# A third PSUM bank pair for the first six score steps, the result added in place, and a remade instruction order

## The chip, the cores and the metric

The kernel runs on one core of a Trainium2 chip. The metric is the time of one execution in microseconds (us), measured on the device. A run also reports the mean clock that TensorE was granted, and a profile shows one execution in detail. Runs marked slow (more than 1.5% above the fastest of their kernel) are left out of every comparison and are named where they occur.

TensorE is called PE below, its weight loads PEld, VectorE DVE, ScalarE ACT, GpSimd POOL, and SyncE SP.

## The reference

Attention in which a query sees only keys of its own hash bucket, followed by a layer norm and a two-layer MLP with a residual:

```python
q_bits = einsum('bhsd,dk->bhsk', q, proj) > 0        # 6 hash bits; the same for k
mask   = bucket(q)[..., None] == bucket(k)[..., None, :]
scores = where(mask, q @ k.T / sqrt(D), -1e9)        # B 4, H 8, S 768, D 64
attn   = softmax(scores)                             # + 1e-9 in the denominator
x      = (attn @ v).transpose(0, 2, 1, 3).reshape(B, S, 512)
xn     = (x - mean) / sqrt(var + 1e-6) * g_ln
out    = x + relu(xn @ w_ch1) @ w_ch2                # 512 -> 2048 -> 512
```

## The kernel before

The program is a list of words. Each is `name.engine.arguments`, and the kernel issues them in exactly that order; each engine takes its own words in order and waits, by semaphores, for data and for free buffers.

```python
for word in ORDER.split():
    name, eng, *args = word.split(".")
    OPS[name](ENGINES[eng], *map(int, args))
```

The attention is cut into 72 steps `s` = 0 to 71: 12 blocks `u` of 256 query rows, two groups of four heads, and three parts of the keys. A step is a score step S (24 matmuls), two exponentials E, and a value step A (16 matmuls). Three steps fill one accumulator, which DVE then normalises into `x` (words `na`, `nb`, `nc`). Two accumulators make a block, whose layer norm (`ce`), transposes (`ft`, `fc`), first MLP layer (F, eight pairs of columns), ReLU (R) and second layer (D, quarters of the hidden size) follow.

```python
def sc(s, h):                       # scores of one half (two heads): two banks
    return ps(f"sc{s}{h}", [P, 2, 512], ("scA", "scB")[h])
def S_(eng, s, h):                  # h = 2: all four heads, both bank pairs
    ...
                    nc.tensor.matmul(sc(s, i // 2)[:, i % 2, ...], lh, rh, ...)
def E_(eng, s, h):
    nc.scalar.activation(E(s)[:, heads(h)], sc(s, h), AF.Exp, scale=EXP_SCALE, bias=bias_sb)
def A_(eng, s, h):
    ...
    acc = ps(f"acc{u}{g}", [P, 2, 512], "acc")
    ...
def warm(eng):                      # 46 matmuls on ones, for the clock
    wp = ps("warm", [P, 2, 512], "acc")
    ...
def pf(eng):                        # the projection, spread over a weight tile
    for i in range(4):
        nc.vector.tensor_copy(pfull[32 * i : 32 * i + 32, :, 32 * i : 32 * i + NB], prj)
def lw1(eng, n):                    # one of eight weight loads (four of each layer)
    nc.gpsimd.dma_start(out=w1_sb[:, :, 512 * n : 512 * n + 512], in_=w1ap[:, :, 512 * n : 512 * n + 512])
```

The kernel's PSUM tiles take eight banks: the pairs `scA`, `scB` and `acc`, and one bank each for `f1` and `f2` (hashes and MLP). A hash group is `tn` (DVE transposes), `ha` (four fp32 matmuls) and `bi` (DVE makes the bits). The list begins:

```
mem.v warm.t lp.a lx.s.0.1.1.3 pmem.p p32.p tn.v.0.1.2 pf.v ha.t.0.1.2 ca.p.0.1.2 lx.s.0.0.0.1 tn.v.0.0.0 ha.t.0.0.0
on.p.1 ca.a.0.0.0 lx.s.0.1.0.1 tn.v.0.1.0 ca.a.0.1.0 lv.s.1.0.0 bi.v.0.1.2 ha.t.0.1.0 bi.v.0.0.0 S.t.2.1 E.a.2.1
S.t.2.0 E.a.2.0 ... S.t.0.1 S.t.0.0 ... S.t.1.1 E.a.1.1 S.t.1.0 ...
```

The softmax here doesn't subtract the row's maximum and nothing guards it: scores larger than these inputs give would overflow.

Of the kernel before, what the change touches and what calls it, by code (L numbers as in the profile page):

```python
# [17 lines left out]
mem.v warm.t lp.a lx.s.0.1.1.3 pmem.p p32.p tn.v.0.1.2 pf.v ha.t.0.1.2 ca.p.0.1.2 lx.s.0.0.0.1 tn.v.0.0.0 ha.t.0.0.0  # L18
on.p.1 ca.a.0.0.0 lx.s.0.1.0.1 tn.v.0.1.0 ca.a.0.1.0 lv.s.1.0.0 bi.v.0.1.2 ha.t.0.1.0 bi.v.0.0.0 S.t.2.1 E.a.2.1
S.t.2.0 E.a.2.0 lx.s.1.0.0.1 tn.v.0.1.1 ca.p.0.1.1 ha.t.0.1.1 tn.v.1.0.0 ca.v.1.0.0 bi.v.0.1.0 S.t.0.1 S.t.0.0  # L20
E.a.0.1 E.a.0.0 ha.t.1.0.0 bi.v.0.1.1 S.t.1.1 E.a.1.1 S.t.1.0 E.a.1.0 lv.s.0.0.4 cv.p.0.0.2 sa.p.0.0.2 sa.p.0.0.1
cv.p.0.0.0 lx.s.1.1.0.3 tn.v.1.1.0 tn.v.1.1.1 ha.t.1.1.0 tn.v.1.1.2 ca.a.1.1.2 sa.p.0.0.0 bi.v.1.0.0 lv.s.1.0.3
bi.v.1.1.0 LX.s.1.0.0 tu.v.1.0.0.3 lg.s on.p.0 A.t.2.1 A.t.0.1 A.t.0.0 ca.p.1.1.0 S.t.3.2 E.a.3.1 E.a.3.0
tu.v.1.0.0.1 ha.t.1.1.1 bi.v.1.1.1 tu.v.1.0.0.2 CA.a.1.0.0.1 ha.t.1.1.2 bi.v.1.1.2 A.t.2.0 ca.p.1.1.1 S.t.4.2
E.a.4.0 lx.s.0.0.1.3 tn.v.0.0.1 sb.p.0.0 su.p.0.0 sp.t.0.0 sc.v.0.0 lw2.p.3 A.t.1.1 tn.v.0.0.2 ha.t.0.0.1 bi.v.0.0.1
lw1.p.3 ca.p.0.0.1 A.t.1.0 na.v.0.0 nb.v.0.0 nc.v.0.0 E.a.4.1 S.t.6.2 E.a.6.0 ha.t.0.0.2 bi.v.0.0.2 lv.s.0.4.4
cv.p.0.4.0 cv.p.0.4.2 A.t.4.2 A.t.3.2 sa.p.0.4.0 sa.p.0.4.2 sa.p.0.4.1 sb.p.0.4 su.p.0.4 lw1.p.0 E.a.6.1 S.t.5.2
E.a.5.0 lx.s.1.0.1.3 tn.v.1.0.1 ca.p.1.0.1 tn.v.1.0.2 ha.t.1.0.1 bi.v.1.0.1 LX.s.1.0.1 tu.v.1.0.1.3 tu.v.1.0.1.1
tu.v.1.0.1.2 LX.s.1.1.0 ha.t.1.0.2 LX.s.2.0.1 bi.v.1.0.2 sp.t.0.4 sc.v.0.4 E.a.5.1 S.t.7.2 E.a.7.1 E.a.7.0 A.t.5.2
na.v.0.1 S.t.8.2 E.a.8.1 E.a.8.0 nb.v.0.1 A.t.7.2 nc.v.0.1 ce.v.0.0 ft.t.0.0 A.t.6.2 ce.v.0.1 ft.t.0.1 fc.a.0.1  # L30
S.t.9.2 E.a.9.1 E.a.9.0 tu.v.1.0.1.0 LX.s.1.1.1 fc.v.0.0 F.t.0.1 F.t.0.6 R.a.0.1 R.v.0.6 A.t.8.2 S.t.10.2 E.a.10.1
E.a.10.0 lw1.p.1 F.t.0.3 F.t.0.2 R.a.0.2 na.v.1.0 nb.v.1.0 A.t.9.2 nc.v.1.0 CA.p.1.0.1.1 lw2.p.0 ca.v.0.0.2 S.t.11.2
E.a.11.0 E.a.11.1 tu.v.1.0.0.0 hm.t.1.0 bt.v.1.0 mo.s.1.0.2.0 mo.s.1.0.3.0 mo.s.1.0.2.1 mo.s.1.0.0.0 A.t.10.2
lv.s.1.0.1 R.v.0.3 ca.v.1.0.2 CA.a.1.0.1.0 tu.v.1.1.0.1 mo.s.1.0.2.2 S.t.13.2 E.a.13.1 E.a.13.0 A.t.11.2 na.v.1.1
nb.v.1.1 nc.v.1.1 ce.v.1.0 fl.s.1.0 lw1.p.2 F.t.0.5 R.v.0.5 F.t.0.4 R.a.0.4 S.t.14.2 E.a.14.0 E.a.14.1 lw2.p.1
F.t.0.0 R.a.0.0 lw2.p.2 A.t.13.2 ce.v.1.1 fl.s.1.1 F.t.0.7 R.v.0.7 mo.s.1.0.1.3 mo.s.1.0.1.0 lv.s.1.4.0 mo.s.1.0.3.3
lv.s.1.0.2 sa.p.1.0.1 sa.p.1.0.2 cv.p.1.0.2 CA.a.1.0.0.0 tu.v.1.1.1.0 tu.v.1.1.1.3 tu.v.1.1.1.2 mo.s.1.0.0.3 rs.p.1
S.t.12.2 E.a.12.1 E.a.12.0 D.t.0.0.0 D.t.0.0.1 D.t.0.0.2 rs.p.0 tu.v.1.1.0.3 F.t.1.2 R.v.1.2 S.t.16.2 E.a.16.1
lv.s.1.4.3 mo.s.1.0.2.3 mo.s.1.0.0.2 mo.s.1.0.0.1 F.t.1.1 R.a.1.1 lv.s.1.4.1 mo.s.1.0.3.2 tu.v.1.1.0.0 mo.s.1.0.1.1
A.t.12.2 E.a.16.0 mo.s.1.0.1.2 mo.s.1.0.3.1 A.t.14.2 tu.v.1.1.0.2 CA.a.1.1.0.1 tu.v.1.1.1.1 hm.t.1.1 bt.v.1.1  # L40
mo.s.1.1.0.3 mo.s.1.1.3.1 mo.s.1.1.0.0 mo.s.1.1.1.2 mo.s.1.1.1.1 mo.s.1.1.0.2 mo.s.1.1.2.2 S.t.15.2 E.a.15.0
E.a.15.1 F.t.1.0 R.v.1.0 D.t.0.0.3 F.t.1.7 R.a.1.7 S.t.17.2 E.a.17.0 E.a.17.1 CA.p.1.1.1.1 F.t.1.5 lv.s.1.4.2
LX.s.2.0.0 na.v.2.0 nb.v.2.0 A.t.16.2 nc.v.2.0 A.t.15.2 Z.v.0.0 mo.s.1.1.3.3 mo.s.1.1.1.3 R.v.1.5 F.t.1.3 R.a.1.3
A.t.17.2 na.v.2.1 nb.v.2.1 nc.v.2.1 ce.v.2.1 fl.s.2.1 ce.v.2.0 fl.s.2.0 mo.s.1.1.0.1 S.t.18.2 E.a.18.0 E.a.18.1
mo.s.1.1.1.0 mo.s.1.1.2.0 F.t.1.4 R.a.1.4 D.t.0.1.0 D.t.0.1.1 D.t.0.1.2 D.t.0.1.3 S.t.19.2 E.a.19.0 mo.s.1.1.2.3
mo.s.1.1.2.1 F.t.1.6 R.a.1.6 Z.v.0.1 D.t.1.0.0 D.t.1.0.1 E.a.19.1 mo.s.1.1.3.0 F.t.2.3 R.a.2.3 cv.p.1.4.2 S.t.20.2
E.a.20.0 CA.v.1.1.0.0 tu.v.2.0.1.1 tu.v.2.0.1.2 tu.v.2.0.1.0 tu.v.2.0.1.3 CA.a.2.0.1.1 cv.p.1.0.0 A.t.19.2 E.a.20.1
mo.s.1.1.3.2 F.t.2.2 R.v.2.2 D.t.1.0.2 D.t.1.0.3 O.s.0.1 O.s.0.2 CA.p.1.1.1.0 tu.v.2.0.0.0 tu.v.2.0.0.1 sa.p.1.0.0
sb.p.1.0 lv.s.2.0.2 su.p.1.0 sa.p.1.4.1 sp.t.1.0 sc.a.1.0 LX.s.2.1.1 on.p.2 cv.p.1.4.0 rs.p.2 S.t.23.2 E.a.23.1
E.a.23.0 F.t.2.4 R.v.2.4 lv.s.2.0.0 A.t.18.2 A.t.20.2 na.v.3.0 lv.s.2.0.1 F.t.2.5 R.a.2.5 O.s.0.0 S.t.21.2 E.a.21.0  # L50
E.a.21.1 lv.s.2.0.3 Z.v.1.0 D.t.1.1.0 nb.v.3.0 nc.v.3.0 F.t.2.1 A.t.23.2 R.v.2.1 S.t.22.2 E.a.22.0 E.a.22.1
sa.p.1.4.2 sa.p.1.4.0 sb.p.1.4 su.p.1.4 sp.t.1.4 sc.v.1.4 lv.s.2.4.0 lv.s.2.4.1 A.t.21.2 D.t.1.1.1 tu.v.2.0.0.3
LX.s.2.1.0 F.t.2.0 R.v.2.0 S.t.24.2 E.a.24.1 CA.v.2.0.0.0 E.a.24.0 A.t.22.2 na.v.3.1 cv.p.2.0.0 LX.s.3.0.0
tu.v.2.0.0.2 LX.s.3.0.1 lv.s.2.4.3 lv.s.2.4.2 F.t.2.6 R.v.2.6 D.t.1.1.2 S.t.28.2 E.a.28.0 E.a.28.1 cv.p.2.0.2
CA.v.2.0.0.1 F.t.2.7 R.a.2.7 D.t.1.1.3 nb.v.3.1 nc.v.3.1 ce.v.3.1 A.t.24.2 fl.s.3.1 S.t.25.2 E.a.25.1 E.a.25.0
ce.v.3.0 fl.s.3.0 cv.p.2.4.0 Z.v.1.1 O.s.1.0 O.s.1.3 O.s.1.1 O.s.1.2 hm.t.2.0 tu.v.2.1.0.1 bt.v.2.0 mo.s.2.0.2.3
mo.s.2.0.2.1 mo.s.2.0.0.1 mo.s.2.0.1.1 tu.v.2.1.0.2 tu.v.2.1.0.0 CA.a.2.1.0.0 mo.s.2.0.1.2 mo.s.2.0.0.2 mo.s.2.0.2.2
D.t.2.0.0 D.t.2.0.1 mo.s.2.0.3.2 mo.s.2.0.0.0 mo.s.2.0.3.3 S.t.26.2 E.a.26.1 E.a.26.0 O.s.0.3 mo.s.2.0.1.3 D.t.2.0.2
D.t.2.0.3 Z.v.2.0 sa.p.2.0.1 F.t.3.2 R.a.3.2 A.t.25.2 CA.a.2.0.1.0 tu.v.2.1.1.0 tu.v.2.1.1.1 S.t.29.2 E.a.29.1
E.a.29.0 cv.p.2.4.2 A.t.26.2 F.t.3.5 R.a.3.5 tab.a na.v.4.0 nb.v.4.0 nc.v.4.0 tu.v.2.1.1.3 D.t.2.1.0 D.t.2.1.1  # L60
S.t.27.2 E.a.27.1 E.a.27.0 F.t.3.0 R.v.3.0 mo.s.2.0.3.0 tu.v.2.1.0.3 CA.a.2.1.0.1 LX.s.3.1.1 D.t.2.1.2 A.t.29.2
F.t.3.3 R.a.3.3 S.t.31.2 E.a.31.0 sa.p.2.0.0 sa.p.2.0.2 lv.s.3.0.0 lv.s.3.0.1 D.t.2.1.3 Z.v.2.1 lv.s.3.0.2 F.t.3.1
R.v.3.1 mo.s.2.0.2.0 A.t.28.2 A.t.27.2 na.v.4.1 nb.v.4.1 nc.v.4.1 ce.v.4.0 E.a.31.1 S.t.30.2 E.a.30.1 E.a.30.0
ce.v.4.1 rs.p.4 fl.s.4.1 F.t.3.7 R.a.3.7 D.t.3.0.0 D.t.3.0.1 rs.p.3 S.t.32.2 E.a.32.0 E.a.32.1 O.s.2.2 F.t.3.6
R.v.3.6 A.t.30.2 A.t.31.2 fl.s.4.0 mo.s.2.0.0.3 F.t.3.4 S.t.34.2 mo.s.2.0.3.1 mo.s.2.0.1.0 tu.v.2.1.1.2 CA.p.2.1.1.1
R.v.3.4 hm.t.2.1 bt.v.2.1 mo.s.2.1.0.1 mo.s.2.1.1.3 mo.s.2.1.2.3 mo.s.2.1.3.3 mo.s.2.1.1.1 tu.v.3.0.0.3 mo.s.2.1.2.2
tu.v.3.0.0.1 E.a.34.0 D.t.3.0.2 F.t.4.5 R.v.4.5 E.a.34.1 A.t.32.2 O.s.2.0 S.t.33.2 E.a.33.0 E.a.33.1 F.t.4.7 R.v.4.7
D.t.3.0.3 Z.v.3.0 F.t.4.1 R.a.4.1 S.t.35.2 E.a.35.0 E.a.35.1 mo.s.2.1.3.2 O.s.2.1 na.v.5.0 nb.v.5.0 nc.v.5.0
D.t.3.1.0 D.t.3.1.1 tu.v.3.0.0.0 mo.s.2.1.1.0 lv.s.3.0.3 F.t.4.3 R.a.4.3 mo.s.2.1.0.0 CA.v.3.0.0.0 A.t.35.2
mo.s.2.1.0.2 S.t.36.2 E.a.36.1 E.a.36.0 tu.v.3.0.0.2 CA.a.3.0.0.1 F.t.4.4 R.v.4.4 mo.s.2.1.0.3 mo.s.2.1.3.1  # L70
mo.s.2.1.1.2 mo.s.2.1.2.0 A.t.34.2 A.t.33.2 mo.s.2.1.3.0 mo.s.2.1.2.1 F.t.4.2 R.a.4.2 S.t.37.2 E.a.37.0 D.t.3.1.2
D.t.3.1.3 F.t.4.0 E.a.37.1 S.t.38.2 E.a.38.0 E.a.38.1 na.v.5.1 nb.v.5.1 A.t.37.2 on.p.3 nc.v.5.1 ce.v.5.0 fl.s.5.0
ce.v.5.1 rs.p.5 fl.s.5.1 A.t.36.2 Z.v.3.1 O.s.3.0 O.s.3.1 O.s.3.3 O.s.3.2 LX.s.3.1.0 R.v.4.0 F.t.4.6 R.v.4.6
D.t.4.0.0 CA.p.2.1.1.0 tu.v.3.0.1.3 S.t.39.2 E.a.39.1 tu.v.3.0.1.0 tu.v.3.0.1.1 CA.p.3.0.1.0 F.t.5.0 R.v.5.0
D.t.4.0.1 D.t.4.0.2 D.t.4.0.3 Z.v.4.0 E.a.39.0 S.t.40.2 E.a.40.0 E.a.40.1 F.t.5.4 R.v.5.4 D.t.4.1.0 A.t.38.2
sb.p.2.0 su.p.2.0 sp.t.2.0 sc.a.2.0 sa.p.2.4.0 sa.p.2.4.1 sa.p.2.4.2 lv.s.3.4.2 na.v.6.0 nb.v.6.0 nc.v.6.0 S.t.41.2
E.a.41.1 F.t.5.6 R.a.5.6 sb.p.2.4 su.p.2.4 D.t.4.1.1 D.t.4.1.2 lv.s.3.4.3 F.t.5.5 R.v.5.5 E.a.41.0 A.t.41.2 S.t.44.2
E.a.44.1 E.a.44.0 sp.t.2.4 sc.v.2.4 D.t.4.1.3 Z.v.4.1 O.s.4.2 O.s.4.0 O.s.4.1 F.t.5.1 R.v.5.1 tu.v.3.0.1.2 A.t.39.2
S.t.43.2 E.a.43.0 E.a.43.1 F.t.5.3 A.t.40.2 D.t.5.0.0 R.v.5.3 F.t.5.2 R.a.5.2 S.t.42.2 E.a.42.0 E.a.42.1 O.s.4.3
# [498 lines left out]
```

## Time and profile before

| what | value | where from |
|---|---|---|
| time | 309.18 us, median of 3 (308.16 to 309.53) | the runs |
| profiled execution | 308.49 us, span 306.8 us | the run with a profile |
| PE busy | 295.2 us, 96% | the page, part 1 |
| first hash / first exponential | 7.50 / 12.59 us | timelines of PE and ACT |
| first MLP pair / second layer | 38.81 / 54.70 us | timeline of PE |

PE's row of busy tenths says that the kernel is bound by PE nearly everywhere, and that only the first 40 us leave something to win. The prediction below shows those lines. One more view, POOL's timeline: its weight loads are issued from 20.61 us on, and those issued at 21.63 and 30.33 us carry the two quarters of the first layer that the first MLP matmuls need.

```profile
21.63 0.77 POOL L332 DMA_DIRECT2D w_sb<-in_moe_w_ch_dram  x1
...
30.33 0.84 POOL L332 DMA_DIRECT2D w_sb<-in_moe_w_ch_dram  x1
```

A row reads: start, length, engine, line, operation, written tile <- source, count.

### The profile page before, as it was taken

How to read it: one execution, taken by the hardware profiler on the slowest of the kernel's cores; microseconds unless marked ns; L12 is line 12 of the kernel's file. 1: busy time of each engine (PE TensorE's matmuls, PEld its weight loads, DVE VectorE, ACT ScalarE, POOL GpSimd, SP SyncE). 2: the span in 40 equal slices, each digit the busy share in tenths (PEclk: the TensorE clock that was granted, in tenths of full speed). 3: DMA queues.
4: the chain of work that ended last, by engine and by line, in shares of the span. 5: the costliest groups of instructions: out<-in, count | busy, mean ns of one | idle time of the engine just before them, and what ended most of it. 6: DMA issues, size and time to landing. Idle time of an engine off the chain costs nothing.

```text
span 306.8 us, 9834 instructions
## 1 busy us (share of the span) xinstructions
PE 295.2 (96%) x4310; PEld 209.2 (68%) x4350; DVE 181.0 (59%) x363; ACT 187.3 (61%) x202; POOL 78.4 (26%) x120
## 2 busy tenths in 40 slices
PE   6999799999999999999999999999999999999994
PEld 6777587676676567667667767776666677775663
DVE  3757948667467575576546858358354467336432
ACT  1597789774777777667565766656555757761000
POOL 3498800062912300401540230206400101001000
PEclk9999999999999999999999999999999999999999
DMA  7989999415299917310722210221500302303022
GB/s 183 330 305 289 256 257 186 92 56 149 59 267 310 166 26 183 55 44 30 200 58 71 65 23 6 59 77 28 88 2 20 87 0 21 86 2 77 28 71 68
DMA packets 30426, 33.58 MB, mean 109 GB/s; under 512 B 15536, under 2 KB 27056, under 8 KB 30384
## 3 DMA queue, kind: packets, MB, share of 16 engines
q1 hardware_dynamic: 25744, 28.47, 35.5%
q0 software_dynamic: 4224, 4.19, 8.3%
q8 instruction: 34, 0.56, 0.8%
q10 hardware_dynamic: 416, 0.30, 0.4%
q14 instruction: 8, 0.07, 0.1%
HBM read 27.53 MB, written 6.29 MB: 110 GB/s over the span
## 4 chain that ended last, share of the span: by engine, by line
PE 90%; DVE 4%; ACT 2%; DMA 1%; issue 1%; DVEq 0%
PE f L498 28%; PE sc L430 18%; PE acc L445 11%; PE hp L395 3%; PE hf L317 3%; ACT E L436 2%; DMA X<-in_k_dram 1%; PE f_20None L514 1%; PE f_81None L514 1%; PE f_100None L514 1%; PE f L514 1%; PE f_61None L514 1%; PE f_31None L514 1%; PE f_00None L514 1%; PE f_70None L514 1%
## 5 line engine op out<-in xcount | busy, mean ns | idle before, releaser
L436 ACT ACTIVATE E<-sc,bias_sb 128x1024 bf16<-128x1024 f32 x144 | 153.3, 1110 | 69.4 <-PE sc L430 66.1
L498 PE MATMUL f<-xnT,w_sb 128*128 128x256 bf16 x768 | 99.3, 273 | 0.1
L498 PEld LDWEIGHTS <-w_sb 128*128 128x128 bf16 x768 | 70.9, 98 | 24.0 <-issue 9.0
L508 DVE TENSOR_SCALAR hb<-f 128x512 bf16<-128x512 f32 x57 | 39.3, 690 | 59.1 <-PE f L498 58.2
L514 PEld LDWEIGHTS <-hb 128*128 128x128 bf16 x400 | 37.6, 98 | 34.5 <-issue 3.6
L430 PE MATMUL sc<-qb,kb 32*128 32x256 bf16 x1152 | 53.7, 267 | 0.0
L430 PE MATMUL sc<-G 6*128 6x256 bf16 x576 | 43.2, 273 | 2.2 <-ACT E L436 1.6
L445 PEld LDWEIGHTS <-E 128*128 128x128 bf16 x1152 | 41.4, 98 | 5.1 <-issue 2.2
L445 PE MATMUL acc<-vaug,E 128*128 128x65 bf16 x1152 | 44.1, 194 | 0.0
L506 ACT ACTIVATE hb<-f 128x512 bf16<-128x512 f32 x39 | 23.2, 596 | 33.5 <-PE f L498 33.5
L476 POOL TENSOR_SCALAR rs<-mv 128x2 f32<-128x2 f32 x12 | 7.1, 593 | 103.5 <-DVE mv L470 103.2
L430 PEld LDWEIGHTS <-kb 32*128 32x128 bf16 x1152 | 31.4, 93 | 1.5
L430 PEld LDWEIGHTS <-G 6*128 6x128 bf16 x576 | 16.3, 91 | 19.4 <-issue 16.2
L248 DVE STREAM_TRANSPOSE T<-X 128x384 f32<-128x384 f32 x48 | 25.4, 557 | 1.3 <-POOL kb L259 0.7
L456 DVE SCALAR_TENSOR_TENSOR acc<-vsB,acc 128x520 f32<-128x520 f32 x24 | 16.7, 698 | 11.4 <-PE acc L445 10.0
L348 POOL CAST vaug<-vn 128x768 bf16<-128x768 f32 x16 | 13.2, 841 | 39.7 <-DMA vn<-in_v_dram 39.7
L358 POOL TENSOR_TENSOR t<-vn 128x256 f32<-128x256 f32 x24 | 17.0, 725 | 24.6 <-DMA vn<-in_v_dram 24.3
L471 DVE SCALAR_TENSOR_TENSOR xc<-x,mv,gB 128x512 bf16<-128x512 f32 x24 | 18.1, 752 | 0.8
L467 DVE BATCH_NORM_STATS2 st<-x 128x6 f32<-128x256 f32 x48 | 18.1, 418 | 0.8
L463 DVE TENSOR_TENSOR x<-acc,rc 128x512 f32<-128x512 f32 x24 | 16.6, 691 | 0.8
L317 PE MATMUL hf<-tp,pfull 128*128 128x256 f32 x48 | 13.9, 431 | 1.3 <-DVE pfull L282 1.3
L317 PEld LDWEIGHTS hf<-tp,pfull 128*128 128x128 f32 x48 | 9.5, 212 | 4.0 <-DVE pfull L282 1.6
(95 smaller groups left out, 229.5 us busy)
## 6 DMA issues: line engine op xcount, KB each, us to landing
out_dram<-res SPq DMA_DIRECT2D x44, 128.0 KB
X<-in_k_dram SPq DMA_DIRECT2D x7, 768.0 KB
vn<-in_v_dram SPq DMA_DIRECT2D x24, 192.0 KB
X<-in_q_dram SPq DMA_DIRECT2D x6, 768.0 KB
w_sb<-in_moe_w_ch_dram POOLq DMA_DIRECT2D x8, 512.0 KB, 12.5
vn<-in_v_dram SPq DMA_DIRECT2D x2, 768.0 KB
G<-B SPq DMA_DIRECT2D x96, 4.5 KB
X<-in_q_dram SPq DMA_DIRECT2D x2, 512.0 KB
```

Source lines behind the costliest of these rows:

```text
L248: nc.vector.transpose(d[:, j], s[:, j, kj0 : kj0 + n])
L317: nc.tensor.matmul(hf(g, t, kp)[:, :256], pfull[:, j], tp(g, t, kp)[:, j], start=(j == 0), stop=(j == 1))
L358: nc.gpsimd.tensor_tensor(t3(b, hs)[:, n], s[:, n], s[:, n + 3], op=AOP.add)
L430: nc.tensor.matmul(sc(s, i // 2)[:, i % 2, 256 * kk : 256 * kk + 256], lh, rh, start=(rep == 0), stop=(rep == 2), skip_group_check=True,)
L436: nc.scalar.activation(E(s)[:, heads(h)], sc(s, h), AF.Exp, scale=EXP_SCALE, bias=bias_sb)
L445: nc.tensor.matmul(acc[:, qt, (D + 1) * i : (D + 1) * (i + 1)], E(s)[:, i, 256 * kk + P * qt : 256 * kk + P * qt + P], vaug(u // 3)[:, 4 * ...
L467: nc.vector.bn_stats(stats(u)[:, qt, g], xt(u)[:, qt, 256 * g : 256 * g + 256])
L471: nc.vector.scalar_tensor_tensor(xc(u)[:, t], xt(u)[:, t], mv(u)[:, t, 0:1], gB, op0=AOP.subtract, op1=AOP.mult,)
L498: nc.tensor.matmul(f1[:, n].rearrange("p (t x) -> p t x", t=2), w1_sb[:, dt, P * nt : P * nt + P], xnT(u)[:, :, dt], start=(dt == 0), stop ...
L506: nc.scalar.activation(hb(u)[:, 2 * p : 2 * p + 2], f1, AF.Relu)
L508: eng.tensor_scalar_max(hb(u)[:, 2 * p : 2 * p + 2], f1, 0.0)
L514: nc.tensor.matmul(f2, hb(u)[:, nt, P * t : P * t + P], w2_sb[:, nt, half(h)], start=(nt == 0), stop=(nt == NNT - 1),)
```

## The change

Its intent: fill the first 40 us. In the first six steps the scores rotate over three bank pairs instead of two, so that PE can write a step while ACT still reads the step before it. The third pair is the accumulators' own. For the first five of these steps no accumulator needs it yet, because the first value step comes after the fifth score step; step 3 borrows it once more, after the first accumulator has been read out and before the second begins.

```diff
+    SC_PAIRS = {2: ("scA", "scB"), 0: ("acc", "scA"), 1: ("scB", "acc"), 4: ("scA", "scB"), 3: ("acc", "scA"), 5: ("scB", "acc")}
     def sc(s, h):
-        return ps(f"sc{s}{h}", [P, 2, 512], ("scA", "scB")[h])
+        return ps(f"sc{s}{h}", [P, 2, 512], SC_PAIRS.get(s, ("scA", "scB"))[h])
     def xt(u):
-        return sb(f"x{u}", [P, 2, DM], F32, "x", 3)
+        return sb(f"x{u}", [P, 2, DM], F32, "x", 4)
-    def res(u):
-        return sb(f"res{u}", [P, 2, DM], F32, "res", 2)
     def E(s):
-        return sb(f"E{s}", [P, 4, 512], BF16, "E", 3)
+        return sb(f"E{s}", [P, 4, 512], BF16, "E", 4)
     def Z_(eng, u, t, h=None):
+        x = xt(u)[:, t, half(h)]
         nc.vector.scalar_tensor_tensor(
-            res(u)[:, t, half(h)], made[f"f2_{u}{t}{h}"], rstd(u)[:, t : t + 1], xt(u)[:, t, half(h)], ...
+            x, made[f"f2_{u}{t}{h}"], rstd(u)[:, t : t + 1], x, op0=AOP.mult, op1=AOP.add,
     ... # the output is stored from x instead of res; a DRAM pool is declared and not used
```

The order is remade from end to end. It now begins as follows (cuts marked): no half steps, the projection tile `pf` before the transposes, two hash groups before the first score step, steps in the order 2, 1, 0, 5, 4, 6, 3, 7, 8, and the first-needed weights (`lw1.p.2`) near the head.

```
lx.s.0.1.1.3 lp.a lx.s.0.0.0.1 on.p.1 mem.v pf.v warm.t tn.v.0.1.2 on.p.0 pmem.p ca.a.0.1.2 ... ha.t.0.1.2 bi.v.0.1.2
... ha.t.0.0.0 bi.v.0.0.0 S.t.2.2 E.a.2.1 E.a.2.0 ... lw1.p.2 ... S.t.1.2 ... S.t.0.2 ... lw1.p.0 ... S.t.5.2 ...
S.t.4.2 A.t.2.2 ... A.t.0.2 ... lw2.p.0 ... A.t.1.2 ... S.t.6.2 ... S.t.3.2 ... lw1.p.1 ... S.t.7.2 ... S.t.8.2 ...
```

Of the 96 ReLUs, 18 also go from DVE to ACT, and some casts change their engine.

## The prediction

> **What bounds the kernel now.** I read the page first, then the busy time by stretch, then the timelines of the first 45 us, engine by engine. The page:
>
> ```profile
> PE 295.2 (96%) x4310; PEld 209.2 (68%) x4350; DVE 181.0 (59%) x363; ACT 187.3 (61%) x202; POOL 78.4 (26%) x120
> PE   6999799999999999999999999999999999999994
> ```
>
> TensorE (PE) is busy in nearly every slice; only the first five slices and the last are not full. The busy time by stretch (columns: length, then busy of PE, PEld, DVE, ACT, POOL, clock, DMA share, GB/s) agrees:
>
> ```profile
> 0.00:10.00 10.00, 7.58 (x52) 6.87 (x53) 4.49 (x14) 2.98 (x3) 2.75 (x14) 1.00 0.80 213
> 30.00:40.00 10.00, 7.94 (x148) 6.22 (x147) 7.35 (x17) 7.61 (x8) 7.18 (x9) 1.00 1.16 254
> 40.00:50.00 10.00, 9.98 (x204) 8.07 (x203) 6.89 (x15) 8.73 (x11) 0.00 (x0) 1.00 1.20 245
> 180.00:200.00 20.00, 19.84 (x343) 13.98 (x341) 12.85 (x26) 12.90 (x15) 2.19 (x3) 1.00 0.17 39
> ```
>
> But "busy" is not work. So I price each block of PE work by its start-to-start time in the PE timeline where it runs undisturbed: a full score step (24 matmuls) 0.77 us, plus 0.10 to switch into it; a value step (16) 0.49; a first-MLP pair (8) 0.87; a quarter of a second-MLP row (4) 0.863; a hash group on fp32 (4) 0.863; a packed hash (32) 1.44. The counts are those of the order list: 72 x 0.87 + 72 x 0.49 + 96 x 0.87 + 92 x 0.863 + 8 x 0.437 (half-wide quarters) + 12 x 0.863 + 6 x 1.44, and about 1.5 for small ones and 0.9 for half steps, is about 286 us. From the first hash (7.50) to the last matmul's end (302.98) there are 295.5. So nearly 10 us are not work, and I ask where. Before the first MLP pair at 38.81 the list holds 24.0 us of work, but 31.3 pass: 7.3 are lost there. The remaining 264 us lose only 2 to 3. What can be won lies in the ramp. PE:
>
> ```profile
> 1.11 5.09 PE L291 MATMUL warm<-ones 128*128 128x128 bf16 x46 [1.11 <-DVE ones L263]
> 7.50 4.27 PE L317 MATMUL hf<-tp,pfull 128*128 128x256 f32 x12 [1.30 <-DVE pfull L282]
> ...
> 34.89 0.29 PE L430 MATMUL sc<-G 6*128 6x256 bf16 x4 [1.61 <-ACT E L436]
> ...
> 38.81 1.92 PE L498 MATMUL f<-xnT,w_sb 128*128 128x256 bf16 x16
> ```
>
> DVE sets the 7.50: it transposes first and builds the projection tile after, though the projection had landed when POOL began to copy it, at 2.55 in POOL's timeline.
>
> ```profile
> 5.17 0.77 DVE L248 STREAM_TRANSPOSE tp<-X 128x256 f32<-128x256 f32 x2 [3.83 <-DMA X<-in_k_dram]
> 5.86 1.58 DVE L282 COPY pfull<-prj 32x12 f32<-32x12 f32 x4
> ```
>
> Then ScalarE (ACT) paces the ramp. Its exponentials (two of 1.11 us per step):
>
> ```profile
> 12.59 4.28 ACT L436 ACTIVATE E<-sc,bias_sb 128x1024 bf16<-128x1024 f32 x4 [2.56 <-PE sc L430]
> 17.46 2.12 ACT L436 ACTIVATE E<-sc,bias_sb 128x1024 bf16<-128x1024 f32 x2 [0.59 <-PE sc L430]
> ...
> 20.61 2.12 ACT L436 ACTIVATE E<-sc,bias_sb 128x1024 bf16<-128x1024 f32 x2
> ...
> 23.66 2.12 ACT L436 ACTIVATE E<-sc,bias_sb 128x1024 bf16<-128x1024 f32 x2 [0.20 <-PE sc L430]
> 26.67 2.12 ACT L436 ACTIVATE E<-sc,bias_sb 128x1024 bf16<-128x1024 f32 x2 [0.89 <-PE sc L430]
> 29.68 2.12 ACT L436 ACTIVATE E<-sc,bias_sb 128x1024 bf16<-128x1024 f32 x2 [0.89 <-PE sc L430]
> 32.72 2.12 ACT L436 ACTIVATE E<-sc,bias_sb 128x1024 bf16<-128x1024 f32 x2 [0.93 <-PE sc L430]
> ```
>
> The starts are 3.0 us apart: 2.12 of exponentials and 0.9 in which ACT waits for the scores. A full score step needs both bank pairs empty and both exponentials need it done, so the two engines take turns.
>
> **What the Trainium skill says.** "Perfetto Trace Analysis", section Optimizing Tensor Performance (Matmuls), wants independent matmul groups to rotate through different PSUM banks so that one group's evacuation overlaps the next one's matmuls; the 0.9 us waits are what its lack costs here. "TensorEngine Tiling (Array Packing)", section PSUM Bottleneck, says that packing speeds up TensorE but not the evacuation: 0.77 us against 2.12 agrees. "TensorE: Matmul & The Clock Gate", Part 1, says that matmuls run at half rate until about 3.4 us of sustained activity in a free-running window. The trace agrees in part: the 46 warm-up matmuls take 107 ns each, the half rate, to the end; after 1.5 us idle the first hashes still go slowly, so that 12 records take 4.2 us where a later four take 0.86. The page's granted clock (1.00) does not show it. On measuring: the first of these pages, under Identifying the Most-Contended Engine, calls matmul busy time a poor measure; hence the pricing above.
>
> **The change part by part.** (1) Projection tile before the transposes: its four copies (1.58) fit between 2.55 and the data at 5.17, so the first hash can start when transposes (0.77) and warm-up end, about 6.0 instead of 7.5: 1.5 us. Hashes then follow the warm-up without a gap and should turn fast sooner: up to 1 us of the 1.6 lost there.
> (2) Only two hash groups stand before the first score step, instead of three: by DVE's row durations (transposes 0.7 each until 7.6, two bit groups of 0.42) the step can start near 8.5, its exponentials near 9.4 instead of 12.59: 3.2 us earlier.
> (3) No half steps: a half costs at least 0.45 on PE against 0.77 for a whole, so 6 x 0.45 - 3 x 0.77 saves 0.4 us.
> (4) Three bank pairs for steps 2, 1, 0, 5, 4, 3: each step shares only one pair with the one before it, so its matmuls run beside the second exponential. Against the old 3.0 us cadence steps 5, 4, 3 and the step after 3 win about 0.9 each, but step 6 still takes turns, and the third pair has to be free of accumulators: value steps wait for the third pair's exponential. I count 2 us.
> (5) Result into x, x 3 to 4 buffers, E 3 to 4: the same 25 DVE operations of 0.75 us, nothing saved on PE. An x tile now lives until its output has landed; in the new order the outputs that free a buffer are issued 7 us of PE work or more before it is written again. I count 0.
> (6) 18 of the 96 ReLUs go from DVE (0.69) to ACT (0.60): ACT 187 to about 198 us, DVE 181 to about 169; both under PE: 0.
> (7) Weight loads start earlier on POOL, near 10 us instead of 20.6, filling a dip in the DMA share.
>
> These overlap and mustn't be added. So I follow ACT from 9.4: five steps at 2.12, 1.5 lost to hash bits, one 1.1 cast, steps 6, 3, 7, 8 at 2.12 with two turns of 0.9: step 8 is done at 9.4 + 19.1 + 1.5 + 1.1 + 1.8 = 33; the layer norm behind steps 5, 3, 4 (about 5.5 us of DVE rows after 27.8) ends at about 33 too. First MLP pair near 33.5 rather than 38.81, with the same work before it (24.2 in the new order): 5.3 us. From this I take back about 0.5 for the next part. From 50 us to the end both orders have the same blocks and PE is full: 0. Tail: last matmul, add, output, as before: 0. Net: -4.8.
>
> **Rivals.** (a) The weights become the wait. The DMA is over 1.0 share from 26 to 50 us; the read bytes queued until the last second-layer chunk, 17.9 MB, took until about 52 us, some 0.36 MB/us. The new order wants its fourth quarter of the second MLP at about 47.5 us of work plus 3.5 lost = 51, with 17.7 MB queued before it, among them a query tile of batch 3 that nothing needs yet. If this binds, 1 to 4 us come back: 306 to 308. For it: the margin is about zero. Against: those bytes start earlier. (b) The accumulators that wait for the lent pair, or DVE's in-order queue (a transpose waiting for late query data holds the bits behind it), eat the overlap: only parts 1 and 3 stay, 306.5. (c) The ramp gains fully, with cold matmuls gone: 7 us, 302. (d) The new order upsets the steady part; 0.2% of 250 us would be 0.5 us, but DMA transposes whose consumer comes too soon could cost 2 to 3: 307.
>
> **Range and chances.** 309.18 - 4.8 = 304.4. Range 301.6 to 307.8: (c) at one end, (a) or (d) at the other. Faster by over 2% means below 303.0, which needs 6.2 of the nearly 10 us that are not work: 0.25. Slower by 2% needs a new stall of 11 us: 0.02. Within: 0.73.
>
> **What would show it.** First hash near 6.0; first exponential near 9.4; the first five steps' exponentials nearly back to back; first MLP pair near 33.5; PE idle in the 30 to 40 stretch gone; from 60 us on PE busy 19.7 or more of each 20. I am wrong if the first MLP pair comes after 36, if PE waits for weights or xnT between 40 and 60 us by over 1 us, or if a steady stretch loses more than before.

## The result, and the profile after

The changed kernel takes 305.04 us, median of 4 runs (303.54 to 305.65). The kernel before took 309.36 (308.16 to 310.14, 4 runs) beside it. The ratio is 0.9857, with a 95% interval of 0.9807 to 0.9906: within 2%. Ratios here are the mean time of one kernel's fast runs over that of the other's in the same rounds, so they are not quite the ratio of the medians quoted.

The page of the changed kernel, then its busy time by stretch with the same columns as in the prediction:

```profile
PE 290.1 (96%) x4307; PEld 204.3 (68%) x4350; DVE 168.9 (56%) x348; ACT 197.0 (65%) x217; POOL 79.7 (26%) x120
PE   7898999999999999999999999999999999999994
```

```profile
0.00:10.00 10.00, 7.77 (x82) 6.71 (x83) 5.78 (x20) 4.82 (x5) 2.06 (x12) 1.00 0.79 253
...
20.00:30.00 10.00, 8.40 (x158) 6.23 (x161) 7.65 (x19) 8.94 (x9) 9.73 (x13) 1.00 1.11 313
30.00:40.00 10.00, 9.60 (x200) 7.75 (x196) 8.95 (x20) 7.44 (x8) 7.59 (x13) 1.00 1.18 252
...
180.00:200.00 20.00, 19.89 (x306) 13.18 (x299) 11.04 (x23) 13.11 (x14) 2.28 (x3) 1.00 0.26 57
```

PE has the same matmuls to do, and is busy for 5.1 us less: a slow matmul and a fast one both count as busy. Its idle time is what it was: 306.8 - 295.2 = 11.6 us before, 301.8 - 290.1 = 11.7 after. The gap in the stretch from 30 to 40 is not closed but has moved: 7.94 has become 9.60 there, while the stretch from 20 to 30 fell from 9.58 to 8.40. The wait of 1.61 us that stood before 34.89 is now one of 1.29 us before 29.80. The stretch from 180 to 200 is as full as it was (19.84 and 19.89); the one from 120 to 140 is less full (19.43, before 19.73). PE's timeline of the changed kernel shows where the beginning went:

```profile
1.11 4.04 PE L290 MATMUL warm<-ones 128*128 128x128 bf16 x46 [1.11 <-DVE ones L262]
5.55 2.03 PE L316 MATMUL hf<-tp,pfull 128*128 128x256 f32 x8 [0.40 <-DVE tp L247]
...
29.80 0.29 PE L429 MATMUL sc<-G 6*128 6x256 bf16 x4 [1.29 <-ACT E L435]
...
34.91 1.04 PE L497 MATMUL f<-xnT,w_sb 128*128 128x256 bf16 x8
...
49.85 3.63 PE L513 MATMUL f_00None<-w_sb,hb 128*128 128x512 bf16 x15
53.31 0.93 PE L497 MATMUL f<-xnT,w_sb 128*128 128x256 bf16 x7
```

The first hash starts at 5.55 instead of 7.50, and eight fp32 hash matmuls take 2.03 us, where twelve took 4.27. The first MLP pair starts at 34.91 instead of 38.81, which is 3.9 us earlier. The second layer starts at 49.85 instead of 54.70, and its four quarters run in 3.46 us (to 53.31) without a wait for weights. ACT's timeline of the changed kernel:

```profile
9.19 2.12 ACT L435 ACTIVATE E<-sc,bias_sb 128x1024 bf16<-128x1024 f32 x2 [0.46 <-PE sc L429]
11.89 4.16 ACT L435 ACTIVATE E<-sc,bias_sb 128x1024 bf16<-128x1024 f32 x4 [0.58 <-PE sc L429]
...
19.55 2.12 ACT L435 ACTIVATE E<-sc,bias_sb 128x1024 bf16<-128x1024 f32 x2 [0.81 <-PE acc L444]
...
22.66 4.16 ACT L435 ACTIVATE E<-sc,bias_sb 128x1024 bf16<-128x1024 f32 x4
27.63 2.12 ACT L435 ACTIVATE E<-sc,bias_sb 128x1024 bf16<-128x1024 f32 x2 [0.81 <-PE acc L444]
30.75 2.12 ACT L435 ACTIVATE E<-sc,bias_sb 128x1024 bf16<-128x1024 f32 x2 [1.00 <-PE sc L429]
```

Two rows hold four exponentials each without a gap: there the rotation works. The wait of 0.81 has a new name: the exponential waits for value matmuls (`acc`), because an E buffer has to come free. After that, where only two pairs are left, a step waits about 0.9 again (1.00 before 30.75). DVE's timeline shows the projection tile now early and short, and the layer norm, which ends close before the first MLP pair:

```profile
2.48 0.70 DVE L281 COPY pfull<-prj 32x12 f32<-32x12 f32 x4 [1.14 <-DMA prj<-in_proj_dram]
...
28.61 0.70 DVE L455 SCALAR_TENSOR_TENSOR acc<-vsB,acc 128x520 f32<-128x520 f32 x1 [1.11 <-PE acc L444]
...
32.22 0.42 DVE L250 TENSOR_SCALAR G<-hf 128x256 bf16<-128x256 f32 x1
...
34.29 0.39 DVE L490 COPY xnT<-ft 128x512 bf16<-128x512 bf16 x1
```

From the end of the value steps (28.51) DVE needs until 34.68. Of that, 0.42 us is a bit group and 0.57 us a transpose for other work, which stand in between. PE is no freer: from 32.92 on it runs without a wait, through step 10's scores and two value steps, to the first MLP pair at 34.91. So DVE and PE arrive within 0.23 us of each other.

### The profile page after: what moved, and what is told of

The parts are those of the page before. It is cut to its first block, busy times and chain, and to the rows that moved or that the text cites. A ratio compares the mean times of both kernels' runs of the same rounds, so it can differ in the third digit from the quotient of the medians.

```text
span 301.8 us, 9814 instructions
## 1 busy us (share of the span) xinstructions
PE 290.1 (96%) x4307; PEld 204.3 (68%) x4350; DVE 168.9 (56%) x348; ACT 197.0 (65%) x217; POOL 79.7 (26%) x120
## 4 chain that ended last, share of the span: by engine, by line
PE 86%; DVE 4%; DMA 3%; ACT 2%; SPq 2%; issue 2%; DVEq 0%; ACTq 0%
PE f L497 28%; PE sc L429 17%; PE acc L444 11%; DMA X<-in_k_dram 3%; ACT E L435 2%; PE hp L394 2%; PE hf L316 2%; PE f_11None L513 1%; PE f_101None L513 1%; PE f L513 1%; PE f_51None L513 1%; PE f_00None L513 1%; PE f_60None L513 1%; PE f_40None L513 1%; PE f_10None L513 1%
## 5 line engine op out<-in xcount | busy, mean ns | idle before, releaser
L505 ACT ACTIVATE hb<-f 128x512 bf16<-128x512 f32 x57 | 33.9, 597 | 41.6 <-PE f L497 41.3
L507 DVE TENSOR_SCALAR hb<-f 128x512 bf16<-128x512 f32 x39 | 26.8, 686 | 52.5 <-PE f L497 52.3
L429 PE MATMUL sc<-qb,kb 32*128 32x256 bf16 x1152 | 52.2, 267 | 0.0
L444 PEld LDWEIGHTS <-E 128*128 128x128 bf16 x1152 | 40.6, 98 | 5.6 <-issue 3.1
L429 PE MATMUL sc<-G 6*128 6x256 bf16 x576 | 41.5, 273 | 2.8 <-ACT E L435 1.8
L444 PE MATMUL acc<-vaug,E 128*128 128x65 bf16 x1152 | 43.3, 194 | 0.2 <-ACT E L435 0.2
L475 POOL TENSOR_SCALAR rs<-mv 128x2 f32<-128x2 f32 x12 | 8.0, 666 | 88.9 <-DVE mv L469 88.6
L429 PEld LDWEIGHTS <-kb 32*128 32x128 bf16 x1152 | 30.2, 93 | 1.5
L316 PE MATMUL hf<-tp,pfull 128*128 128x256 f32 x48 | 12.8, 398 | 0.5 <-DVE tp L247 0.4
L258 POOL CAST kb<-T 128x768 bf16<-128x768 f32 x7 | 5.8, 830 | 24.0 <-DVE T L247 24.0
```

Of the source, the lines that this page charges most:

```text
L316: nc.tensor.matmul(hf(g, t, kp)[:, :256], pfull[:, j], tp(g, t, kp)[:, j], start=(j == 0), stop=(j == 1))
L429: nc.tensor.matmul(sc(s, i // 2)[:, i % 2, 256 * kk : 256 * kk + 256], lh, rh, start=(rep == 0), stop=(rep == 2), skip_group_check=True,)
L444: nc.tensor.matmul(acc[:, qt, (D + 1) * i : (D + 1) * (i + 1)], E(s)[:, i, 256 * kk + P * qt : 256 * kk + P * qt + P], vaug(u // 3)[:, 4 * ...
L505: nc.scalar.activation(hb(u)[:, 2 * p : 2 * p + 2], f1, AF.Relu)
L507: eng.tensor_scalar_max(hb(u)[:, 2 * p : 2 * p + 2], f1, 0.0)
```

## The experiments

Two theories stood against each other. By the first, the gain is a sum of separable parts: an earlier start, the lent pair, no halves, earlier weights. By the second, several limits lie side by side before the first MLP pair, and removing one alone brings nothing. Each kernel below was timed in five rounds (6 runs with the profiled one) beside the kernel before, whose medians in the three batches were 308.31, 308.26 and 308.74 us (11 runs each). "Changed" means an edit of the changed kernel, "old" an edit of the kernel before. All results were correct.

| edit | median us | ratio to before [95%] |
|---|---|---|
| changed, none | 305.29 | 0.9902 [0.9855, 0.9949] |
| changed, no lent pair | 309.37 | 1.0040 [0.9996, 1.0084] |
| changed, first-needed weights late | 310.27 | 1.0065 [1.0016, 1.0114] |
| changed, one warm-up matmul | 308.58 | 0.9987 [0.9945, 1.0028] |
| changed, projection tile late | 305.62 | 0.9903 [0.9862, 0.9943] |
| changed, two steps in halves | 305.16 | 0.9920 [0.9870, 0.9971] |
| changed, gaps filled | 306.69 | 0.9919 [0.9881, 0.9957] |
| old, result in place | 308.66 | 1.0010 [0.9969, 1.0050] |
| old, projection tile early | 310.06 | 1.0033 [0.9986, 1.0079] |
| old, 60 warm-up matmuls | 309.07 | 1.0023 [0.9986, 1.0060] |
| old, weights in order of use | 308.63 | 1.0000 [0.9961, 1.0038] |
| old, tile early and weights in order | 308.63 | 0.9985 [0.9947, 1.0023] |

### The changed kernel again

No edit.

> The changed kernel once more, as the measure for the three other runs of this call. 4 us under the kernel before, ratio 0.986. Its own runs spread by 2 us earlier; I expect the same spread, and if it comes from when the matmul clock turns fast, the profile will show the warm-up matmuls or the first hashes at the half rate in slower runs.

It took 305.29 us (304.17 to 308.36). In its profile, of a run of 305.27 us, the first exponential starts at 9.59, the first MLP pair at 35.31 and the second layer at 50.24. So the profile above, of the fastest run (303.54), shows the beginning about 0.4 us better than this one: its warm-up reached full rate at 3.86 us, this one's at 6.48. The larger part of the difference lies late, in a wait that the first profile does not have. PE of this run:

```profile
198.64 1.05 PE L497 MATMUL f<-xnT,w_sb 128*128 128x256 bf16 x8 [1.11 <-DMA xnT<-xc]
```

PE waits 1.11 us for a DMA transpose of the layer norm's output. From the start of the second layer to PE's last matmul this run takes 249.3 us, the first profile 248.1 and the kernel before 248.3. Four other fast traces of the new order wait at this place too (0.50 to 1.27 us), and the run without the lent pair does not; in the five fast traces of the old order no wait for such a transpose is over 0.56. So the new order gives back about 1 us there in most traces. Why the transpose comes late was not tested.

The gain was 3.0 us of median here and 4.3 us at first; the two intervals overlap.

### Without the lent pair

```diff
-    SC_PAIRS = {2: ("scA", "scB"), 0: ("acc", "scA"), ...}
+    SC_PAIRS = {}
```

> The changed kernel with two bank pairs for all steps, order untouched: the lending alone undone. If the overlap of scores and exponentials in the first six steps is what the change gains, each of steps 1, 0, 5, 4, 3, 7 waits for both exponentials of the one before it again, about 0.9 us each where ACT has nothing else, while value steps no longer wait for the lent pair: 2 to 4 us slower than the changed kernel (307 to 309), first MLP pair near 37 to 38. Rival (the order and the early start are the gain, the lending is not): under 0.7 us slower.

It took 309.37 us (309.11 to 311.82), 4.1 more than the changed kernel and no better than the kernel before. The turn-taking is back. ACT of this run, then one of PE's waits for it:

```profile
19.44 2.12 ACT L435 ACTIVATE E<-sc,bias_sb 128x1024 bf16<-128x1024 f32 x2 [0.92 <-PE sc L429]
22.39 2.12 ACT L435 ACTIVATE E<-sc,bias_sb 128x1024 bf16<-128x1024 f32 x2 [0.83 <-PE sc L429]
26.10 2.12 ACT L435 ACTIVATE E<-sc,bias_sb 128x1024 bf16<-128x1024 f32 x2 [1.59 <-PE acc L444]
```

```profile
34.42 0.29 PE L429 MATMUL sc<-G 6*128 6x256 bf16 x4 [1.13 <-ACT E L435]
```

The profiled run, the slowest of the six, had bad luck besides: a load came late, so that its first exponential started at 12.27, and 3.4 us of half clock followed. So take only the stretch from the first exponential to the start of step 8's: 39.07 - 12.27 = 26.8 us here, 30.75 - 9.19 = 21.6 in the changed kernel. Of the 5.2 us between them some 1.4 are the half clock (eight hash matmuls in 3.42 us instead of 1.99), by an estimate from these two rows. The other 3.8 are the bank pairs, which agrees with the 4.1 of the times. In this order the lent pair is worth about 4 us. That is not what it wins over the kernel before: there the same nine steps, from the first exponential to the start of step 8's, take 35.87 - 12.59 = 23.3 us, so the changed kernel is 1.7 faster, and the new order without the pair is slower than the old one, by about 2 us at full clock. The old order cut its first three steps in halves, which the new one gave up. Halves in place of the lent pair were not tried in the new order.

### The first-needed weights late

The eight loads keep their places in the list, but their contents are shifted, so that `lw1.p.2` goes out at about 27 us instead of 10.

```diff
- lw1.p.2  lw1.p.0  lw2.p.0  lw1.p.1  lw1.p.3  lw2.p.1  lw2.p.2  lw2.p.3     # the places in the list, in order
+ lw2.p.3  lw1.p.0  lw2.p.0  lw1.p.2  lw1.p.1  lw1.p.3  lw2.p.1  lw2.p.2
```

> The changed kernel with the weight quarter that its first MLP pair needs asked for near 27 us instead of 10 (the last quarter of the second layer takes the early place). If the early weight loads are part of the gain, which I had counted as 0, the first MLP pair waits for weights until 36 to 39 us and the whole is 1 to 3 us slower than the changed kernel. Rival (it lands in time): within 0.4 us.

It took 310.27 us (308.55 to 313.0), about 5 more than the changed kernel, well over what was expected. PE of this run:

```profile
38.55 1.05 PE L497 MATMUL f<-xnT,w_sb 128*128 128x256 bf16 x8 [3.44 <-DMA w_sb<-in_moe_w_ch_dram]
```

PE waits 3.44 us for the weights, though they went out 11.6 us before they were there. Then, from 39.47 to 42.88, PE's clock is at half, and 16 MLP matmuls take 2.86 us instead of 1.92. By an estimate from this trace, 3.4 of wait and half of 3.4 at half rate make 5.1. So loading these weights earlier than at 27 us is a necessary part of the gain.

### Weights in order of use, in the old order

```diff
- lw2.p.3  lw1.p.3  lw1.p.0  lw1.p.1  lw2.p.0  lw1.p.2  lw2.p.1  lw2.p.2
+ lw1.p.0  lw1.p.3  lw1.p.1  lw1.p.2  lw2.p.0  lw2.p.1  lw2.p.2  lw2.p.3
```

> The kernel before with its weight loads in the order in which they are used, at the same places in POOL's order: the first quarter of the first layer is asked for at 20.6 us instead of 30.3. Alone I expect little, 0 to 0.7 us faster, because in the profile of before the first MLP pair waited for the layer norm and the copy behind it, not for weights.

It took 308.63 us (307.64 to 310.32): nothing. PE does not wait for weights before the first MLP pair in this trace (39.58) nor in the kernel before (38.81), so there was nothing for earlier weights to win. Together with the two runs above this shows limits side by side: weights early without the lent pair give a ratio of 1.0040 (new order) and 1.0000 (old order), the lent pair without the weights gives 1.0065, and both together 0.9902. The lent pair in the old order was not run.

### The start alone, in the old order: two runs that missed

```diff
- ... pmem.p p32.p tn.v.0.1.2 pf.v ha.t.0.1.2 ...
+ ... pmem.p p32.p pf.v tn.v.0.1.2 ha.t.0.1.2 ...
```

> The kernel before with its projection tile made before the first transposes: that part alone. First hash at 6.0 instead of 7.5; if the start carries through, 1 to 1.5 us faster than before, more where the hashes also turn fast sooner. Rival (the turn-taking of scores and exponentials or the loads set the first MLP pair): under 0.5 us.

The projection tile early should have saved 1 to 1.5 us. It took 310.06 us (308.32 to 313.46, the highest a slow run): no gain. The first hash did start at 5.99 instead of 7.50, but the next load came late and the first exponential started at 11.50, 1.1 earlier. The first MLP pair came at 39.05, no earlier at all, and it waited 0.36 us for its weights.

```diff
-NWARM = 46
+NWARM = 60
```

> The kernel before with 60 warm-up matmuls instead of 46, which fills the 1.5 us that PE idles before the first hash at no cost. If the slow clock costs there, the 12 first hash records take 2.6 to 3.5 us instead of 4.27 and the whole is 1 to 1.7 us faster. Rival (the first hashes aren't on the path): the records faster, the time the same within 0.5.

Sixty warm-up matmuls: 309.07 us (308.25 to 310.64), again no gain. The twelve hash matmuls took 2.90 us instead of 4.27, and the exponentials ran 1.4 us ahead of those of the kernel before. Then, from 34.98 on, PE ran at half clock for 6.8 us, and the lead was gone:

```profile
38.62 3.46 PE L498 MATMUL f<-xnT,w_sb 128*128 128x256 bf16 x16
```

The kernel before ran that row in 1.92 us. The next run's trace helps to see where the half clock comes from.

### The result in place, alone, and the half clock

```diff
-        return sb(f"x{u}", [P, 2, DM], F32, "x", 3)
+        return sb(f"x{u}", [P, 2, DM], F32, "x", 4)
-    def res(u): ...                       # and every res(u) becomes xt(u)
```

> The kernel before with the result added into the x tile and 4 x buffers, its order untouched: that part alone. I expect nothing: within 0.5 us of before (ratio 0.998 to 1.002). Rival (freed memory and fewer tiles matter by themselves, or the longer life of x stalls DVE): over 1 us either way, with DVE waiting for output transfers in the second case.

It took 308.66 us (307.63 to 310.79): nothing, as expected. Its profile happens to be an early start: PE turned to full rate at 6.78 us instead of 10.41, and the first exponential came 1.16 us earlier. Yet the first MLP pair came only 0.47 earlier. The trace's clock records are multiples of 3.41 us long. So I cut each trace into steps of 3.41 us from its first record on, and read PE's busy time and clock in each. First this run, then the kernel before, then the changed kernel, each around its longest wait of PE for the exponentials:

```profile
30.68:34.09 3.41, 1.80 (x56) 1.54 (x57) 3.20 (x8) 2.12 (x2) 3.41 (x5) 1.00 1.07 297
34.09:37.50 3.41, 3.41 (x60) 2.86 (x48) 3.08 (x8) 2.12 (x2) 1.95 (x3) 0.50 1.24 207
```

```profile
30.89:34.30 3.41, 2.39 (x45) 1.66 (x44) 3.26 (x8) 2.48 (x3) 3.38 (x5) 1.00 1.07 304
34.30:37.71 3.41, 2.37 (x61) 1.92 (x61) 3.28 (x8) 2.38 (x3) 2.90 (x5) 1.00 1.20 202
```

```profile
27.75:31.17 3.42, 2.13 (x66) 1.88 (x63) 2.42 (x6) 2.42 (x3) 3.01 (x3) 1.00 1.13 288
31.17:34.58 3.41, 3.04 (x61) 2.32 (x59) 3.21 (x8) 2.47 (x3) 1.63 (x3) 1.00 1.11 308
```

The first number after the length is PE's busy time, and the third from the end the clock. In this run the wait of 1.61 us falls into one window: PE is busy for 1.80 and idle for 1.61, and the next window runs at 0.50. In the profiled run of the kernel before the same wait is cut in two by the border at 34.30. The windows are idle for 1.02 and, with a further wait of 0.42, for 1.04, and the clock stays. In the changed kernel the longest wait is 1.29 and lies wholly in one window, and the clock stays too.

In the twelve traces of fast runs, leaving out the last 8 us of each, there are seven full-rate windows that a half-rate one follows, with 1.39 to 2.92 us of PE idle in them; the largest idle time in a window that no half-rate one follows is 1.37. (In the last 8 us one window with 1.47 was followed by full rate.) So the old order stands on the edge: its wait of 1.61 costs a window of half clock or not, as the grid falls, and an earlier start only moves the wait against the grid. This reading is taken from those traces, and each of them fits it; it was not tested by an experiment of its own.

The runs without a profile agree, though they do not show where in the run a half window lay. Of 33 runs of the kernel before in these batches, 19 have a mean clock of 0.994 or less, and one half window of 3.41 us in 307 takes 0.0056 off it. Of ten runs of the changed kernel as it is, one has: the slowest, at 308.36 us and 0.992. Still, the clock is the smaller part. The 14 runs of the kernel before at 0.997 or more average 308.3 us, and the nine of the changed kernel 305.1, so 3.2 us remain at the same clock.

### Early tile and weights together, in the old order

The order edits of the two runs above in one kernel, which leaves the old bank pairs as they are.

> The kernel before with the projection tile first and the weight loads in order of use. With the projection tile alone the first MLP pairs waited 0.36 and 0.52 us for weights and nothing was gained. If the weights took the gain back, those waits go and the whole is 0.7 to 1.5 us faster than before. Rival (the half-rate window near 34 us, in which the profiles of two variants of before fell, takes it back): the waits go, the time is within 0.5 us of before and most runs show a mean granted clock of 0.994 or less.

It took 308.63 us (306.77 to 312.84, the highest a slow run), ratio 0.9985: nothing. Not one of the six runs had a clock above 0.994. The profile fell on the slow run, so its trace isn't used. The expectation's rival had foreseen this clock. But the clock does not hide a gain: the four runs at 0.993 or 0.994 average 308.05, twelve runs of the kernel before at that clock 308.40. This is the strongest run for the second theory: of the parts, tile and weights are there, and without the bank pairs and the rest of the order they are worth nothing that can be measured.

### The start, in the new order

```diff
- ... mem.v pf.v warm.t tn.v.0.1.2 ...
+ ... mem.v warm.t tn.v.0.1.2 pf.v ...
```

> The changed kernel with the projection tile made after the first transposes, as before. If the first hash's start carries through the ramp, it comes 0.7 to 1.5 us later (the four copies) and the whole is 0.7 to 1.5 us slower. Rival (later waits, the layer norm or the DMA, set the first MLP pair): first hash late, but the first MLP pair within 0.3 us of 34.9 and the time the same.

With the tile late the median is 0.3 us higher (305.62, 305.25 to 306.8), and the ratio is the same as without the edit. Both the expected 0.7 to 1.5 us and its rival missed: the first hash starts at 6.58 instead of the repeat's 5.99, and the first MLP pair at 36.03 instead of 35.31, 0.7 later, but part of that comes back at the late wait for a transpose, 0.75 us here and 1.11 there. Here the four copies take 0.66 us, not the 1.58 they took in the kernel before. There they ran beside a cast on POOL (6.08 to 7.12 us), which the new order has moved to ACT.

```diff
-NWARM = 46
+NWARM = 1
```

> The changed kernel with 1 warm-up matmul in place of 46. If the slow clock at the start costs, the first 8 to 16 hash matmuls take 427 ns instead of 216: 1.7 us or more lost before the first scores, 1 to 3 us slower. Rival (PE has slack there, DVE and ACT pace the start): under 0.5 us slower.

Without the warm-up it took 308.58 us (306.49 to 309.29), 3.3 more. PE reaches the full clock at 14.71 us; PE of this run:

```profile
5.61 3.78 PE L316 MATMUL hf<-tp,pfull 128*128 128x256 f32 x8 [4.21 <-DVE tp L247]
```

Those eight matmuls take 2.03 us in the changed kernel. The first MLP pair comes at 38.82 instead of the repeat's 35.31. So the warm-up is worth 3 us where nothing later gives it back. Both kernels have it, so this is no part of the gain.

### Two steps in halves again

```diff
- S.t.8.2 ... S.t.10.2
+ S.t.8.1 S.t.8.0 ... S.t.10.1 S.t.10.0
```

> The changed kernel with score steps 8 and 10, the first two after the lent ones that still take turns with the exponentials, cut into head halves. If turn-taking is what remains in the ramp, ACT's waits of 0.8 to 1.0 us before the exponentials of steps 8 and 10 fall to about 0.3, PE pays 0.1 each, and the whole is 0.5 to 1.5 us faster than the changed kernel. Rival (the layer norm on DVE sets the first MLP pair, and PE has nothing else to do): within 0.3 us.

Where only two pairs are left, halves could stand in for the rotation. It took 305.16 us (304.72 to 308.7): the same as the changed kernel. ACT of this run:

```profile
27.63 4.22 ACT L435 ACTIVATE E<-sc,bias_sb 128x1024 bf16<-128x1024 f32 x4 [0.82 <-PE acc L444]
33.58 2.12 ACT L435 ACTIVATE E<-sc,bias_sb 128x1024 bf16<-128x1024 f32 x2 [1.73 <-PE sc L429]
```

The wait of 1.00 before step 8 is gone, and the one before step 10 has grown from 0.94 to 1.73. The first MLP pair comes at 34.93, as before the edit (34.91). So that wait alone does not set this point. Step 8's scores end when they did (30.64), because their second half waits for step 7's exponentials; step 10's scores now wait 0.15 us for DVE's bits; PE then runs without a wait to the first MLP pair; and DVE's last `xnT` copy ends at 34.68 as before. ACT, DVE and PE's own order lie side by side there, and no run separates them.

### A try at filling the gaps

The changed kernel with three steps in halves, one hash group and its bits moved forward, the hash into the wait of 1.29, and step 9 before the first MLP pair:

```diff
- A.t.4.2 E.a.7.0 S.t.8.2 ... ha.t.1.0.1 ... S.t.10.2 ... F.t.0.4 R.a.0.4 S.t.9.2 E.a.9.1 E.a.9.0
+ A.t.4.2 ha.t.1.0.1 E.a.7.0 S.t.8.1 S.t.8.0 ... S.t.10.1 S.t.10.0 ... S.t.9.1 S.t.9.0 F.t.0.4 E.a.9.1 R.a.0.4 E.a.9.0
```

> The changed kernel with steps 8, 10 and 9 in halves, the hash for step 10 moved into PE's wait of 1.29 us before step 8, its bits ahead of the layer norm's end, and step 9 ahead of the first MLP pair. If PE's idle time behind steps 5, 3, 4 (1.7 us) is only for want of work whose inputs are ready, 0.7 to 1.5 us faster than the changed kernel. Rival (the bits and the layer norm on DVE set everything there): within 0.4 us.

It took 306.69 us (304.66 to 310.24, the highest a slow run), ratio 0.9919: not better than the changed kernel. Its profile fell on the slow run, so why is open. No version beat the changed kernel.

## Why the prediction was right

The time is 305.04 against 304.4 predicted, inside the range and in the class that was given the highest chance. Step by step:

- **The bound and the place of the gain: right.** The first profile shows 5.0 us won, 3.9 of them by the first MLP pair and 4.9 by the second layer. The repeat's profile has 3.5 and 4.5 at these points, and 3.2 at the end.
- **Following ACT: right.** Predicted were the first exponential at 9.4 and step 8 done at 33; the trace has 9.19 and 32.87. Of the two turns of 0.9 us that were counted, one came (1.00); in the other's place is a wait of 0.81 for value matmuls.
- **The first MLP pair: too early.** The value steps were to end at 27.8 and the layer norm to take 5.5 us, with the first MLP pair at 33.5. The value steps ended at 28.51, DVE's rows took 6.1 with the bits and the transpose between them, and the pair came at 34.91. So 3.9 us were won here instead of 5.3.
- **Part (1), 1.5 us for the tile and up to 1 for the clock: the tile was too large.** In the new order its place is worth 0.3 us of time and 0.7 by the first MLP pair, in the old order nothing. The long copies go with the cast beside them. The clock's share can be read only from the profiles, and it changes from run to run: the first twelve hash matmuls of the kernel before take 4.2 us from start to start instead of 2.6 at their full pace, and the first eight of the changed kernel 1.9 instead of 1.7. (The prediction reads PE's idle time before these as 1.5 us; the row says 1.30.)
- **Part (2), 3.2 us from two hash groups, part (3), 0.4 from whole steps, and part (6), 0 for the ReLUs:** the first exponential came 3.4 us earlier, and ACT and DVE are busy for 197.0 and 168.9 us, as forecast. None of the three had an experiment of its own.
- **Part (4), 2 us for the bank pairs: near, a little large.** Against the kernel before, the nine steps up to step 8 are 1.7 us shorter, with part (3) in it, for which 2.4 were counted together. The 4.1 that the pair costs when it is taken out is another quantity: what the new order, which gave up the halves, loses without it.
- **Part (5), 0 for the result in place: right** (308.66 against 308.26).
- **Part (7), 0 for the weights: right alone, wrong in the sum.** Early weights bring nothing in the old order, but asked for at 27 us in the new one they cost 5. The prediction called them the filling of a dip; they are what lets the other parts count.
- **Rival (a): refuted.** The second layer's fourth quarter came without a wait. **Rival (b)** is seen in small: exponentials wait 0.81 twice for value steps, but the overlap was not eaten. **Rival (c), 302, is not reached:** the first MLP pair came only 3.9 us earlier. **Rival (d)** is absent from the first profile, but in the repeat it came in small: the wait of 1.11 us for a transpose at 198.64.
- **What it did not see:** that the 1.61 us wait of the kernel before sits at the edge of a half-clock window. So "the same work, started earlier" was no sure gain in the old order.

The prediction warned that its parts overlap and followed ACT instead of adding them, and this is why its path holds. That the first result is so near to 304.4 is partly luck. Two misses had opposite signs: by the first MLP pair 1.4 us less was won than counted, and from there to the second layer 1.0 more, where 0.5 was to be given back (about half of the 1.0 is work that the new order does before the first MLP pair). And the gain of 4.3 us in the first result was 3.0 in the repeat, against 4.8 forecast. Open are what the new order would cost with three E buffers, what the lent pair would do in the old order, why the transpose near 198 us comes late, and whether the grid of the clock could be met on purpose.

## What to carry to other kernels

Where two waits lie side by side in front of the same instruction, removing either one measures as nothing: test the parts by taking them out of the finished version, not only by adding them to the old one. But what a part costs when it is taken out (here 4.1 us) need not be what it won over the old version (here 1.7 or less). A buffer that is idle during the ramp, here the accumulators' banks, can break a turn-taking of two engines for as long as it is idle. And a wait of TensorE that looks harmless can be followed by a stretch of half clock, so read the clock window by window before calling a lead lost for unknown reasons.

## What the Trainium skill lacked or had wrong

- "TensorE: Matmul & The Clock Gate", Part 1, has the array go back to half rate after an idle window of about 3.4 us, and its rule is to leave no idle gap longer than that. The window length agrees (records of 3.41 us), but here no idle window was needed: windows with 1.39 to 2.92 us of PE idle were followed by half rate, and a wait of 1.61 us was enough when 1.39 or more of it fell inside one window. The same part does report, as a second failure mode, that frequent short idle times bring half rate too; it gives no size for them.
- The same page says that the turn to full rate takes about 3.4 us of sustained work and depends on the phase. The runs show how wide this is: with the same 46 warm-up matmuls, the first at 1.11 us, full rate began between 3.86 and 6.98 us in six traces of the new order, so from 2.75 us of work on, and at 4.09, 6.78 and 10.41 in three of the old order, where PE is idle for 1.3 to 2.1 us after the warm-up.
- "Perfetto Trace Analysis", Optimizing Tensor Performance (Matmuls), advises rotating through PSUM banks and gives no worth for it: here taking the third pair out cost 4.1 us of 305, and having it brought nothing when the weights came late. It does not say that banks of a later stage can be lent.
- "SBUF — State Buffer", Who interferes with whom, says that a DVE copy in a two-port mode and a GpSimd instruction lock each other out for a whole instruction. Nothing is lacking here, and these runs fit it: four small DVE copies took 1.58 us beside a POOL cast of 1.04, and 0.66 without it.
